# Two chained matmul steps taken in turn, one scaling write instead of two, and weight preparation moved by some ticks, in a fused attention and mixer kernel

## The chip, the cores and the metric

One core of a Trainium2 chip runs the whole program in one launch. The metric is device microseconds for one execution (lower is better), as the median of several runs. The engines are TensorE (PE in the profile, with PEld for its weight loads), VectorE (DVE), ScalarE (ACT), GpSimd (POOL) and SyncE (SP), which issues most of the DMAs.

## What is computed

The inputs are float32: q, k and v of shape (2, 8, 768, 64) and the weights of two feed-forward blocks. The reference, cut to what matters here (the attention's output x has the shape (2, 768, 512)):

```python
# 1. attention: a query sees the keys whose six hash bits (signs of q @ proj, k @ proj) are its own
scores = np.where(q_bucket == k_bucket, q @ k.T / 8, -1e9)
x = softmax(scores) @ v
# 2. first block: token shift, then
k = np.maximum(xk @ w_k, 0)
x = sigmoid(xr @ w_r) * (k * k @ w_v)
# 3. second block: gating along the sequence
h = np.maximum(x @ w_in, 0)
u, v = h[..., :512], h[..., 512:]
v_n = (v - v.mean(-1)) / np.sqrt(v.var(-1) + 1e-6)
v_s = w_spatial @ v_n + b_spatial[:, None]
out = (u * v_s) @ w_out
```

## The kernel before

Every float32 operand of a matmul is held as two fp32r parts, a high part (a cast, made by ACT) and a low part (operand less high part, a subtraction by DVE). A product is then three matmuls, high by high, high by low and low by high; `mm3` (L178) writes them for a list of chunks of 128 rows. A product over 512 rows is a group of 12 matmuls of 512 columns.

The program has two parts. `attention` issues its work in an order written out by hand (L578). `mixers` does both feed-forward blocks, and its order is set by ticks: each call of a group of matmuls ends in `tick()` (L200), which advances a counter and issues the jobs that stand in the plan for that tick, in the order in which they were put there. `at_tick(n, job)` plans a job; `later(lag, job)` plans one relative to now. All engines run their own instructions in the order of issue, so a job's tick sets its place in the queue of its engine, not its time.

The first block ends at tick 59. The second block treats the 1536 rows of x as three tiles n = 0, 1, 2 of 512 rows. It has these steps:

- `step_u(n)` (L916): four groups for the half u of `x @ w_in`, each evacuated by ACT with a Relu into XT (L920). Ticks 60 to 63 for n = 0, 64 to 67 for n = 1, 76 to 79 for n = 2.
- `step_w(n)` (L923): four groups for the half v, each evacuated by ACT into a tile `vt` (two buffers), followed by the statistics on DVE (L939, L940) and, issued at the same tick's end, `scale` (L947): a square root on ACT (L948), a reciprocal (L949) and the normalising write on DVE (L953). Ticks 68 to 75 for n = 0 and 1, 80 to 83 for n = 2.
- `step_s(b, i)` (L962): seven products of 9 matmuls of 384 columns for the mixing along the sequence, by a scheme that forms sums and differences of quarters of the operands and so needs seven block products instead of eight. Then `step_o(b, hf)` (L1020): the output products, and the DMA of the result.

The order before is u(0), u(1), w(0), w(1), u(2), w(2), then s and o (L1092 to L1134). The work that it needs is planned around it:

- `plan_split(n, ticks)` (L648) makes the operand of tile n from XT: the high part (L651, ACT) at a tick and the low part (L655, DVE) one tick later, for four chunks c. There are eight slots: tile n uses the slots 4 * (n % 2) to 4 * (n % 2) + 3, so tile 2 takes the slots of tile 0 over and can be written when both u(0) and w(0) have read them.
- `plan_in(1, ticks)` (L710) prepares the second half of `w_in`, which step w reads, in four chunks of 128 rows. `plan_weight` (L205) spreads a chunk over ticks: the load (L38) two ticks ahead, the magnitude (L42, ACT) at its tick n, clamp, shift and top (L45, L50, L56, DVE) at n + 1, first (L72, ACT), power and low (L63, L66, DVE) at n + 2, and rest (L77, L78, DVE), which writes the low half of the weight, at n + 3. The raw words lie in `w_raw`, which has two buffers: the load of chunk c waits for the low job of chunk c - 2.
- `plan_spatial(c, n)` (L826) prepares a third of `w_spatial`: two loads at n - 2 (L833) into the same two buffers of `w_raw`; at n a copy by ACT (L843) and five subtractions by DVE (L846 and L850 to L853, the plain low part and the differences of quarters); at n + 2 two copies by ACT (L860, highs) and two subtractions by DVE (L864, lows). The loads of the next third wait for these lows, one for each buffer.
- `plan_quarter` (L874) loads two more quarters of `w_spatial` at ticks 79 and 82.
- `first_part` to `seventh_part` (L1046 to L1077) form the operands of step s from the normalised quarters, at ticks 74 to 81 for batch 0 and between the groups of step o for batch 1.

The normalised v of batch b is held in four quarters a11, a12, a21 and a22 (`raw_tile`, L756, six buffers of 128 x 2 x 384). One group of step w gives 128 rows of two of them; `scale` writes them in two operations, one for each quarter, with 256 columns each. The results of matmuls go to six PSUM banks in turn (`bank`, L169).

Of the kernel before, what the change touches and what calls it, by code (L numbers as in the profile page):

```python
# [10 lines left out]
F32 = mybir.dt.float32  # L11
# [7 lines left out]
HS = S // 2  # L19
# [612 lines left out]
def mixers(tc, nc, mid, wide, top, XT, slots, parked, epsT, wr, wk, wv, w_in, w_spT, b_sp, w_out, out, split,  # L632
# [15 lines left out]
    def plan_split(n, ticks):  # L648
        for c, t in enumerate(ticks):
            def first(c=c):  # L650
                nc.scalar.copy(slots[4 * (n % 2) + c][:, 0], own(n, c))  # L651

            def rest(c=c):
                d = slots[4 * (n % 2) + c]
                nc.vector.tensor_sub(d[:, 1], own(n, c), d[:, 0])  # L655

            at_tick(t, first)
            at_tick(t + 1, rest)
# [6 lines left out]
    with tc.tile_pool(name="m1", bufs=1) as m1:  # L665
        more = m1.tile([128, 2, 2, TB], F32R, name="more")
        slots.extend(more[:, n] for n in range(2))
        k2, os, held = {}, {}, []

        def step_r(n):  # L670
            for m in range(4):
                r_group(n, m, m1, "rg", 2)

        def k_bank(i):
            if i % 4 == 3:
                return obank
            return ps_t.tile([128, 512], F32, tag="t", name="k")

        def key(i):
            n, m = divmod(i, 8)  # L680
            o = k_bank(i)
            mm3(o, [(wsl(wk, c, m), hl(slots[4 * (1 - n % 2) + c])) for c in range(4)])
            t = m1.tile([128, TB], F32, tag="kt", name="kt")
            nc.scalar.activation(t, o, AF.Relu)
            nc.scalar.square(t, t)
            k2[i] = m1.tile([128, 2, TB], F32R, tag="k2", bufs=4, name="k2")
            nc.scalar.copy(k2[i][:, 0], t)  # L687
            held.append(lambda kk=k2[i]: nc.vector.tensor_sub(kk[:, 1], t, kk[:, 0]))  # L688
            if m != 1 or n == 0:
                held.pop()()  # L690
            tick()

        def value(i):
            n, c = divmod(i, 8)
            if c == 0:
                os[n] = [ps_s.tile([128, 2, 512], F32, tag="s", name="v") for _ in range(2)]
            xh, xl = hl(k2.pop(i))
            for m in range(4):
                o = os[n][m // 2][:, m % 2, :]
                wh, wl = wsl(wv[c // 4], c % 4, m)  # L700
                for k, (w, x) in enumerate(((wh, xh), (wh, xl), (wl, xh))):
                    nc.tensor.matmul(o, w, x, start=(c == 0 and k == 0), stop=(c == 7 and k == 2))  # L702
                if c == 7 and m % 2:
                    for k in (m - 1, m):
                        nc.vector.tensor_mul(own(n, k), os[n][k // 2][:, k % 2, :], rg[n][:, k, :])
            while held:
                held.pop()()
            tick()

        def plan_in(h, ticks):  # L710
            for c, t in enumerate(ticks):
                w = wk[:, :, c, DM:] if h else wr[:, :, c, :]
                plan_weight(t, hl(w), w_in[128 * c:128 * c + 128, DM * h:DM * h + DM])

        def new_w_out():
            w_o.append(top.tile([128, 2, 2, DM], F32R, tag="x", name="w_o"))

        def plan_out(cs, ticks):
            for c, t in zip(cs, ticks):
                plan_weight(t, lambda c=c: wo(c), w_out[128 * c:128 * c + 128])  # L720

        plan_mix(2, 0, 0, (2, 3, 4, 5), nc.vector)
        plan_mix(0, 1, 4, (6, 7, 8, 9), nc.vector)
        plan_mix(1, 1, 0, (13, 15, 18, 20), nc.scalar)
        plan_in(0, (28, 31, 34, 37))
        at_tick(39, new_w_out)
        plan_out((0, 1), (40, 43))
        plan_mix(2, 1, 4, (29, 32, 35, 38), nc.scalar)
        plan_split(0, (45, 46, 47, 48))
        plan_out((2, 3), (48, 51))  # L730
        plan_in(1, (54, 56, 58, 60))
        plan_split(1, (57, 58, 60, 61))
        gates()
        r_group(0, 2, top)
        r_group(0, 3, top)
        step_r(1)
        step_r(2)
        assert now[0] == 11
        key(0)
        key(1)  # L740
        for i in range(24):
            if i < 22:
                key(i + 2)
            value(i)
        assert now[0] == 59

    with tc.tile_pool(name="m2", bufs=1) as m2:
# [5 lines left out]
        vop = {k: m2.tile([128, 2, 2, HS], F32R, name=f"v_{k}") for k in ("a11", "a12", "a22")}  # L753
        raw, w22, b11, work = {}, {}, {}, {}

        def raw_tile(dt=F32):  # L756
            return m2.tile([128, 2, HS], dt, tag="raw", bufs=6, name="raw")

        def wide_op(t, i):
            if i:  # L760
# [3 lines left out]
        def op_of(k, b, i):  # L764
            if k in vop:
                return vop[k][:, 0, i], vop[k][:, 1, i]
            if k == "s1":
                return one[:, 0, i], one[:, 1, i]
            if k == "s2":
                if b == 0:  # L770
                    t = parked[6 + i]
                elif i:
                    t = parked[3]
                else:
                    t = work["s2"]
                return t[:, 0], t[:, 1]
            return wide_op(wr if k == "s3" else wk, i)

# [137 lines left out]
        def step_u(n):  # L916
            for m in range(4):
                o = bank("u")
                mm3(o, [(wsl(wr, c, m), hl(slots[4 * (n % 2) + c])) for c in range(4)])
                nc.scalar.activation(plain(n, m), o.rearrange("p (h s) -> p h s", h=2), AF.Relu)  # L920
                tick()

        def step_w(n):  # L923
            for j in range(4):
                o = bank("w")
                js = slice(128 * j, 128 * j + 128)
                pairs = []
                for c in range(4):
                    xh, xl = hl(slots[4 * (n % 2) + c])
                    pairs.append(  # L930
                        ((xh[:, js], xl[:, js]), (wk[:, 0, c, DM:], wk[:, 1, c, DM:]))
                    )
                mm3(o, pairs)
                t = m2.tile([128, DM], F32, tag="vt", bufs=2, name="vt")
                nc.scalar.activation(t, o, AF.Relu)
                st = m2.tile([128, 6], F32, tag="st", bufs=3, name="st")
                mv = m2.tile([128, 2], F32, tag="mv", bufs=3, name="mv")
                sd = m2.tile([128, 1], F32, tag="sd", bufs=3, name="sd")
                nc.vector.bn_stats(st, t)  # L939
                nc.vector.bn_aggr(mv, st)  # L940
                b, c = divmod(4 * n + j, 6)
                names = ("a12", "a22") if c > 2 else ("a11", "a21")
                if b == 0 and c == 0:
                    for k in ("a11", "a12", "a21", "a22"):
                        raw[0, k] = raw_tile()

                def scale(t=t, mv=mv, sd=sd, b=b, c=c, names=names):  # L947
                    nc.scalar.activation(sd, mv[:, 1:2], AF.Sqrt, bias=epsT)  # L948
                    nc.vector.reciprocal(sd, sd)  # L949
                    for h, k in enumerate(names):  # L950
                        if (b, k) not in raw:
                            raw[b, k] = raw_tile()
                        nc.vector.tensor_scalar(  # L953
                            raw[b, k][:, :, 128 * (c % 3):128 * (c % 3) + 128],
                            t[:, 256 * h:256 * h + 256].rearrange("p (i n) -> p i n", i=2),
                            mv[:, 0:1], sd, op0=ALU.subtract, op1=ALU.mult,
                        )

                later(1, scale)
                tick()  # L960

# [96 lines left out]
        def fourth_part(b):  # L1058
            low("s1", b)
            s2_sum(b)  # L1060
            low("a11", b)
            for i in range(2):
                high("s2", b, i)
# [13 lines left out]
                low("s3", b, i)  # L1077

        for c in range(3):
            plan_spatial(c, (64, 66, 69)[c])  # L1080
        plan_split(2, (71, 72, 73, 73))
        h21, l21, _ = plan_quarter(lambda t, c: wr[:, t, c, :HS], 0, 79)
        h22, l22, s22 = plan_quarter(lambda t, c: wk[:, t, c, DM:DM + HS], HS, 82)
        for n, job in zip(
# [5 lines left out]
        at_tick(82, l21)  # L1090
        turn[0] += 1
        step_u(0)  # L1092
        step_u(1)
        step_w(0)
        step_w(1)
        step_u(2)
        step_w(2)
        assert now[0] == 83
        t = raw_tile()
        work.update(a=t[:, 0], b=t[:, 1], u=s22[1][:, HS:])  # L1100

        def before_first():
# [8 lines left out]
        step_s(0, 0, before_first, within_first)  # L1111
        step_s(0, 1, middle=lambda: low("s4", 0, 1))

        def more_sums():
            work["s2"] = raw_tile(F32R)
            fourth_part(1)

        def last_sums():
            for i in range(2):
                high("s4", 1, i)  # L1120
# [6 lines left out]
            fifth_part(1)  # L1127

        step_o(0, 0, (lambda: first_part(1), lambda: second_part(1), lambda: third_part(1)))
        step_o(0, 1, (more_sums, next_sums, last_sums))  # L1130
        step_s(1, 0)
        step_s(1, 1)
        step_o(1, 0)
# [67 lines left out]
```

## Time and profile before

| | |
|---|---|
| median of 3 runs | 535.88 us (532.23 to 537.28) |
| the profiled execution | 530.72 us, span 528.6 us |
| PE busy in it | 520.0 us, 98% of the span |
| DVE busy | 416.9 us, 79% |
| ACT busy | 331.6 us, 63% |
| POOL busy | 148.2 us, 28% |
| granted clock of TensorE | 1.0 over the span |

The profile is of one execution. Its span runs from the first instruction to the last, and the time of the execution has some 2 us around it. The rows further down are from its trace: each names an engine, a line of the kernel, the operation, output and input tile, and times in us from the start of the span. A value in brackets with an arrow is the time that the engine sat idle before that instruction, and what released it. An engine's instructions overlap a little where the next one doesn't read what the last one wrote, so the distance of two starts can be less than a duration.

### The profile page before, as it was taken

The page shows a single profiled execution, that of the slowest core. Times are in us where ns is not written, and L with a number is a line of the kernel's source. Part 1 is how long each engine was busy: PE and PEld are TensorE (multiplying, and loading weights), DVE is VectorE, ACT ScalarE, POOL GpSimd, SP SyncE. Part 2 cuts the span into 40 slices and gives each one's busy share as a digit, 9 for nine tenths or more (in the row PEclk, how much of TensorE's full clock was granted, in tenths as well). Part 3 has the DMA queues.
Part 4 walks back from the last instruction along what each step waited for, and adds up shares of the span by engine and source line. Part 5 has one row for each costly group of instructions (what it writes and reads, how often), then busy time and mean ns, then how long its engine had stood idle before and what let it go on. Part 6 is the DMA issues. An engine that isn't in the chain of part 4 may idle for free.

```text
span 528.6 us, 8305 instructions
## 1 busy us (share of the span) xinstructions
PE 520.0 (98%) x2850; PEld 417.1 (79%) x2850; DVE 416.9 (79%) x861; ACT 331.6 (63%) x682; POOL 148.2 (28%) x159
## 2 busy tenths in 40 slices
PE   8999999999999999999999999999999979999997
PEld 6778676868677776688888888888888858998996
DVE  8787898888989789989678687856885898977750
ACT  8888788878788687566666567554444455326121
POOL 7859766776785441100000000000000000210300
PEclk9999999999999999999999999999999999999999
DMA  8986876686859310301211121212221200103002
GB/s 237 190 181 145 191 192 139 151 196 180 165 141 171 90 64 16 96 1 41 79 55 66 42 79 42 79 40 81 80 91 60 91 14 1 46 1 116 5 20 101
DMA packets 20042, 49.88 MB, mean 94 GB/s; under 512 B 3776, under 2 KB 7424, under 8 KB 20000
## 3 DMA queue, kind: packets, MB, share of 16 engines
q1 hardware_dynamic: 14288, 32.35, 20.2%
q0 software_dynamic: 5280, 16.71, 15.1%
q8 instruction: 23, 0.38, 0.3%
q10 hardware_dynamic: 432, 0.28, 0.2%
q14 instruction: 19, 0.16, 0.1%
HBM read 45.11 MB, written 3.19 MB: 91 GB/s over the span
## 4 chain that ended last, share of the span: by engine, by line
PE 86%; DVE 6%; DMA 5%; ACT 2%; issue 1%; SPq 0%; DVEq 0%; ACTq 0%
PE v L702 12%; PE o L183 12%; PE o L462 11%; PE t L427 11%; PE s L395 11%; PE k L183 9%; PE s L183 7%; PE r L183 6%; PE u L183 4%; PE w L183 2%; DVE p L405 1%; DMA rb<-ds 1%; DMA wst<-in_w_spT_dram 1%; DMA w_raw<-in_w_r_dram 1%; DMA x<-in_kq_dram 1%
## 5 line engine op out<-in xcount | busy, mean ns | idle before, releaser
L405 DVE TENSOR_SCALAR_CACHE_REDUCE p<-s 128x768 f32<-128x768 f32 x96 | 91.2, 952 | 17.0 <-PE s L395 11.9
L417 ACT ACTIVATE p<-p,m 128x768 f32<-128x768 f32 x96 | 90.1, 940 | 13.8 <-DVE p L405 12.9
L395 PE MATMUL s<-tk 128*128 128x384 f32 x384 | 87.0, 357 | 0.1
L131 POOL TENSOR_TENSOR tk<-g,tk 128x384 fp32r<-128x384 f32 x8 | 9.2, 1155 | 273.8 <-ACT tk L130 270.1
L427 PEld LDWEIGHTS t<-ident,p 128*128 128x128 f32 x576 | 65.8, 140 | 19.7 <-ACT p L417 4.9
L427 PE MATMUL t<-ident,p 128*128 128x128 f32 x576 | 80.2, 276 | 0.7 <-ACT PT L433 0.4
L433 ACT COPY PT<-t 128x384 f32<-128x384 f32 x146 | 64.7, 475 | 21.4 <-PE t L427 21.4
L702 PE MATMUL v<-k,wv 128*128 128x512 f32 x288 | 68.9, 389 | 0.0
L462 PE MATMUL o<-PT,v 128*64 128x384 f32 x384 | 66.4, 492 | 0.4 <-DVE XT L474 0.4
L395 PEld LDWEIGHTS s<-tk 128*128 128x128 f32 x384 | 62.6, 189 | 2.7 <-POOL tk L341 0.6
L702 PEld LDWEIGHTS v<-k,wv 128*128 128x128 f32 x288 | 54.1, 188 | 11.2
L276 POOL TENSOR_TENSOR tk<-x,tk 64x384 fp32r<-64x384 f32 x56 | 57.8, 1051 | 10.8 <-DMA tk<-in_kq_dram 9.5
L462 PEld LDWEIGHTS o<-PT,v 128*64 128x64 f32 x384 | 25.8, 137 | 31.6 <-issue 30.2
L688 DVE TENSOR_TENSOR k<-kt,k 128x512 fp32r<-128x512 f32 x24 | 16.6, 690 | 24.8 <-ACT k L687 24.6
L183 PE MATMUL k<-tk,wk 128*128 128x512 f32 x144 | 35.6, 389 | 0.0
L183 PEld LDWEIGHTS k<-tk,wk 128*128 128x128 f32 x144 | 27.0, 188 | 5.6
L130 ACT CAST tk<-g 128x384 fp32r<-128x384 f32 x16 | 8.2, 513 | 36.4 <-DVE g L973 36.4
L156 DVE SCALAR_TENSOR_TENSOR f<-XT,msc,d 128x256 f32<-128x256 f32 x48 | 24.1, 503 | 6.5 <-ACT d L150 5.1
L183 PE MATMUL w<-wk,tk 128*128 128x512 f32 x114 | 26.5, 389 | 0.0
L433 DVE COPY PT<-t 128x384 f32<-128x384 f32 x46 | 24.7, 547 | 2.1 <-PE t L427 2.0
L183 PE MATMUL r<-tk,wr 128*128 128x512 f32 x108 | 25.7, 392 | 0.0
L183 PEld LDWEIGHTS w<-wk,tk 128*128 128x128 f32 x114 | 21.4, 188 | 4.4
(194 smaller groups left out, 933.5 us busy)
## 6 DMA issues: line engine op xcount, KB each, us to landing
tk<-in_kq_dram POOLq DMA_DIRECT2D x30, 384.0 KB, 7.8
x<-in_kq_dram POOLq DMA_DIRECT2D x6, 768.0 KB, 5.0
w_raw<-in_w_k_dram SPq DMA_DIRECT2D x8, 512.0 KB
w_raw<-in_w_v_dram SPq DMA_DIRECT2D x8, 512.0 KB
w_raw<-in_w_in_dram SPq DMA_DIRECT2D x8, 512.0 KB
v<-in_vP_dram SPq DMA_DIRECT2D x8, 384.0 KB
rb<-ds SPq DMA_DIRECT2D x30, 96.0 KB
out_dram<-ot SPq DMA_DIRECT2D x11, 256.0 KB
```

Of the source, the lines that this page charges most:

```text
L131: (eng or nc.vector).tensor_sub(lo, src, hi)
L156: nc.vector.scalar_tensor_tensor(st["f"], x, mu, st["d"], op0=ALU.mult, op1=ALU.add)
L183: nc.tensor.matmul(o, a, x, start=(i == 0), stop=(i == len(seq) - 1))
L276: nc.gpsimd.tensor_sub(tk[l, 1 + 2 * t, o], raw[pp][l, t, o], tk[l, 2 * t, o])
L395: nc.tensor.matmul(s[:, c, :HS], w, t[:, n, c * HS:(c + 1) * HS], start=(n == 0), stop=(n == 1),)
L405: nc.vector.tensor_scalar(c, s[:, :, :HS], -0.125, BIG / 16, op0=ALU.mult, op1=ALU.min, accum_out=m)
L417: nc.scalar.activation(c, c, AF.Exp, bias=m, scale=-1.0, accum_out=den[g][:, u:u + 1])
L427: nc.tensor.transpose(t[:, 128 * n:128 * n + 128], p[:, k0:k0 + 128], ident)
L433: copy(PT[g][:, e, 3 * c:3 * c + 3, 128 * j:128 * j + 128], t[:, :HS].rearrange("p (n q) -> p n q", n=3),)
L462: nc.tensor.matmul(obank[64 * e:64 * e + 64, :HS], vt[g // 2][:, kt, e, :], PT[g][:, e, kt, :], start=(kt == 0), stop=(kt == 5),)
L688: held.append(lambda kk=k2[i]: nc.vector.tensor_sub(kk[:, 1], t, kk[:, 0]))
L702: nc.tensor.matmul(o, w, x, start=(c == 0 and k == 0), stop=(c == 7 and k == 2))
```

## The change

The steps u and w alternate: u(0), w(0), u(1), w(1), u(2), w(2). The plan follows: the last chunk of the second half of `w_in` comes a tick earlier, the splits of tile 1 come four ticks later, those of tile 2 one or two ticks earlier (three of the four), and the second and third part of the spatial weights one and two ticks later. The normalised quarters of one group lie side by side in one tile of four (three buffers of double size), and one operation of 512 columns writes what two of 256 wrote. The scratch of step s is the half of such a tile that held a12 of batch 0, and the first s2 operand of batch 1 lies in a parked slot instead of a raw tile.

```diff
@@ mixers @@
-        plan_in(1, (54, 56, 58, 60))
-        plan_split(1, (57, 58, 60, 61))
+        plan_in(1, (54, 56, 58, 59))
+        plan_split(1, (61, 62, 64, 65))
...
-        def raw_tile(dt=F32):
-            return m2.tile([128, 2, HS], dt, tag="raw", bufs=6, name="raw")
+        def raw_tile():
+            return m2.tile([128, 4, HS], F32, tag="raw", bufs=3, name="raw")
@@ op_of @@
                 if b == 0:
                     t = parked[6 + i]
-                elif i:
-                    t = parked[3]
                 else:
-                    t = work["s2"]
+                    t = parked[1 + 2 * i]
@@ step_w @@
-                if b == 0 and c == 0:
-                    for k in ("a11", "a12", "a21", "a22"):
-                        raw[0, k] = raw_tile()
-
                 def scale(t=t, mv=mv, sd=sd, b=b, c=c, names=names):
                     nc.scalar.activation(sd, mv[:, 1:2], AF.Sqrt, bias=epsT)
                     nc.vector.reciprocal(sd, sd)
-                    for h, k in enumerate(names):
-                        if (b, k) not in raw:
-                            raw[b, k] = raw_tile()
-                        nc.vector.tensor_scalar(
-                            raw[b, k][:, :, 128 * (c % 3):128 * (c % 3) + 128],
-                            t[:, 256 * h:256 * h + 256].rearrange("p (i n) -> p i n", i=2),
-                            mv[:, 0:1], sd, op0=ALU.subtract, op1=ALU.mult,
-                        )
+                    if c % 3 == 0:
+                        raw[b, c] = raw_tile()
+                        for h, k in enumerate(names):
+                            raw[b, k] = raw[b, c][:, 2 * h:2 * h + 2]
+                    nc.vector.tensor_scalar(
+                        raw[b, c - c % 3][:, :, 128 * (c % 3):128 * (c % 3) + 128],
+                        t.rearrange("p (k n) -> p k n", k=4),
+                        mv[:, 0:1], sd, op0=ALU.subtract, op1=ALU.mult,
+                    )
@@ mixers @@
-            plan_spatial(c, (64, 66, 69)[c])
-        plan_split(2, (71, 72, 73, 73))
+            plan_spatial(c, (64, 67, 71)[c])
+        plan_split(2, (69, 70, 72, 73))
...
         step_u(0)
+        step_w(0)
         step_u(1)
-        step_w(0)
         step_w(1)
         step_u(2)
         step_w(2)
         assert now[0] == 83
-        t = raw_tile()
+        t = raw[0, "a12"]
...
-        def more_sums():
-            work["s2"] = raw_tile(F32R)
-            fourth_part(1)
...
-        step_o(0, 1, (more_sums, next_sums, last_sums))
+        step_o(0, 1, (lambda: fourth_part(1), next_sums, last_sums))
```

## Rows read from the trace of the kernel before

**Rows 1.** The page, busy time of each engine over the span.
```profile
PE 520.0 (98%) x2850; PEld 417.1 (79%) x2850; DVE 416.9 (79%) x861; ACT 331.6 (63%) x682; POOL 148.2 (28%) x159
```

**Rows 2.** Waits of PE: who waited for whom, us in total, times, longest.
```profile
PE u L183 <- DVE tk L655: 2.7, 3, 1.3
PE o L285 <- POOL ident masks.py:199: 1.3, 1, 1.3
```

**Rows 3.** PE in order of time, 375 to 452 us: start, us, engine, line, what.
```profile
379.51 2.88 PE L183 MATMUL u<-tk,wr 128*128 128x512 f32 x12
382.24 2.88 PE L183 MATMUL o<-tk,wr 128*128 128x512 f32 x12
...
423.04 0.39 PE L183 MATMUL u<-tk,wr 128*128 128x512 f32 x1
423.60 0.97 PE L183 MATMUL u<-tk,wr 128*128 128x512 f32 x3 [0.17 <-DVE tk L655]
425.84 0.96 PE L183 MATMUL u<-tk,wr 128*128 128x512 f32 x3 [1.27 <-DVE tk L655]
428.08 6.90 PE L183 MATMUL u<-tk,wr 128*128 128x512 f32 x29 [1.28 <-DVE tk L655]
...
448.42 1.75 PE L183 MATMUL s<-b,v_a 128*128 128x384 f32 x9
```

**Rows 4.** DVE in order of time, 365 to 456 us.
```profile
374.57 0.69 DVE L66 SCALAR_TENSOR_TENSOR w_a<-w_raw,w_p 128x512 f32<-128x512 uint32 x1
...
379.29 0.68 DVE L655 TENSOR_TENSOR tk<-XT,tk 128x512 fp32r<-128x512 f32 x1
...
391.31 0.68 DVE L655 TENSOR_TENSOR wk<-XT,wk 128x512 fp32r<-128x512 f32 x1
...
392.64 0.69 DVE L78 TENSOR_TENSOR wk<-w_b,w_a 128x512 fp32r<-128x512 f32 x1
...
404.76 0.56 DVE L846 TENSOR_TENSOR b<-wst,b 128x384 fp32r<-128x384 f32 x1 [2.83 <-ACT b L843]
...
407.61 0.69 DVE L939 BATCH_NORM_STATS2 st<-vt 128x6 f32<-128x512 f32 x1
...
408.43 1.80 DVE L864 TENSOR_TENSOR wsp<-wst,wsp 128x768 fp32r<-128x768 f32 x2
...
410.40 0.73 DVE L953 TENSOR_SCALAR raw<-vt,mv,sd 128x256 f32<-128x256 f32 x2
...
422.89 0.66 DVE L655 TENSOR_TENSOR tk<-XT,tk 128x512 fp32r<-128x512 f32 x1
...
425.12 0.66 DVE L655 TENSOR_TENSOR tk<-XT,tk 128x512 fp32r<-128x512 f32 x1
...
427.36 1.26 DVE L655 TENSOR_TENSOR tk<-XT,tk 128x512 fp32r<-128x512 f32 x2
...
441.14 0.70 DVE L939 BATCH_NORM_STATS2 st<-vt 128x6 f32<-128x512 f32 x1 [1.12 <-ACT vt L935]
```

**Rows 5.** ACT in order of time, 365 to 456 us.
```profile
378.88 0.68 ACT L42 ACTIVATE w_a<-w_raw 128x512 f32<-128x512 f32 x1
...
404.22 0.51 ACT L843 CAST b<-wst 128x384 fp32r<-128x384 f32 x1 [3.41 <-DMA wst<-in_w_spT_dram]
...
412.33 0.51 ACT L843 CAST b<-wst 128x384 fp32r<-128x384 f32 x1 [1.68 <-DMA wst<-in_w_spT_dram]
```

**Rows 6.** The chain that ended last, 380 to 530 us: start, us, what.
```profile
401.09 3.10 DMA wst<-in_w_spT_dram
...
409.38 2.93 DMA wst<-in_w_spT_dram
```

**Rows 7.** DVE's groups by line and shape: count, busy us, mean ns, idle before.
```profile
L45 DVE TENSOR_SCALAR w_a<-w_a 128x512 f32<-128x512 f32 x32 | 15.6, 489 | 0.0
...
L953 DVE TENSOR_SCALAR raw<-vt,mv,sd 128x256 f32<-128x256 f32 x24 | 8.8, 410 | 0.4
...
L152 DVE TENSOR_SCALAR d<-XT,omu 128x256 f32<-128x256 f32 x24 | 8.4, 349 | 0.4
```

## The prediction

> **What bounds the kernel now.** I read the page's busy shares first: PE is busy for 520.0 of 528.6 us and every other engine for less than 80% [rows 1]. Where PE never rests, only two things can shorten the run: less work for PE, or the removal of a wait of PE. The change takes no matmul away, so the second view is the list of what PE waited for. Its longest entry is 2.7 us, in three waits of the products u for the subtraction at L655, the split of the operand tiles; the next is 1.3 us, in the matmuls that warm PE at the start (L285), and what follows is smaller still [rows 2].
>
> The third view, PE in order of time, places them. A group of 12 matmuls takes 2.72 us: the first starts at 379.51, the second at 382.24 [rows 3]. Steps u and w are 24 such groups, so 65.3 us without a wait, and step s would start at 379.51 + 65.3 = 444.8. It starts at 448.42 [rows 3]. The 3.6 us lost all lie in the first group of step u(2): 1, 3 and 3 matmuls stand at 423.04, 423.60 and 425.84, each piece ending in a wait for one more chunk's low half, and from 428.08 PE runs on without a pause [rows 3]. (The list gives 2.7 us because the matmul before a wait is drawn longer than its place in the pipe; the starts give the whole loss.)
>
> The fourth view, DVE in order of time, says why the splits are late. The four of tile 2 are written at 422.89, 425.12, 427.36 and straight after, between statistics and scalings of w(1) [rows 4]. DVE runs from 404.76 to there almost without a pause; the wait before 404.76 was 2.83 us for ACT [rows 4], which itself stood 3.41 us for a load of the spatial weights, and again 1.68 us before 412.33 [rows 5]. The two loads took 3.10 and 2.93 us from the release of their buffer [rows 6]. So DVE has the work of eight w groups and of spatial chunks 1 and 2 pressed into the 20 us before u(2), and PE overtakes it there. It catches up later: at 441.14 it waits 1.12 us for ACT in the first group of w(2) [rows 4]. After that PE shows no wait to the end [rows 2], so a microsecond saved before u(2) is a microsecond of the whole.
>
> **The new order.** w(0) comes before u(1). Tile 0's slots are then free after group 8 instead of 12 and can take tile 2 four groups earlier, and w(0)'s work for DVE moves from 404 on to 394 on. I walk DVE's queue in the new order with the durations of the trace, PE's groups at 2.72 us from 379.51. (The same walk over the order of before starts s at 448.3 against 448.42, so the method is good to about 0.2 us.)
>
> **Weights for w(0).** They are wanted 10.9 us earlier: w(0) starts at 379.51 + 4 x 2.72 = 390.39, and its eleventh matmul, the first that reads the low half of chunk 3, at 392.66. Before, that half was written from 392.64 to 393.33, behind an unbroken queue which held four splits of tile 1, the first at 379.29 and the last at 391.31 [rows 4]. The change puts those splits behind it. Four times 0.60 is 2.4 us, so it is done at 390.9 to 391.1, 1.6 us in hand. The magnitude of chunk 3 is a tick earlier on ACT. Its load still waits for chunk 1's product to free a buffer, which ends just after 379.3, where the split follows it [rows 4]. A load of this size took 3.6 us at most (chunk 0's product ends at 374.57 + 0.69, chunk 2's magnitude starts at 378.88) [rows 4, 5], so the magnitude runs from 383.0, and DVE comes to it at 385.7. ACT stands there for about 3.5 us with the evacuation of u(0)'s first group behind it; PE has six banks in turn and is 16 us from wanting that one back. Cost: nothing. If the load took over 7.2 us, PE would wait for the excess.
>
> **Splits of tile 1.** All four now end by 401.9 in the walk; u(1) starts at 401.27 and wants the last low half at its eleventh matmul, 403.5. In hand 1.6 us, cost nothing.
>
> **The merged scaling.** Two 128x256 writes take 0.73 us together [rows 4], 0.41 each [rows 7]. No row shows one of 128x512 with two per-partition scalars. Lower bound 0.42, the clamp at that size with immediates, in this stretch (its mean over the run is 0.49 [rows 7]). Upper bound 0.81: 0.69 for the statistics over the same 512 columns [rows 4], plus 0.12 for two scalars (0.41 against 0.35 for the form with one gives 0.06 each [rows 7]). I take 0.54: 0.41 less 0.12 is 0.29 for 256 columns with immediates, against 0.42 for 512, so 256 more columns cost 0.13. It is nearest to the clamp, the same operation on the same kind of operand. The gain is 0.2 us in each of 12 groups, all on DVE.
>
> [...]
>
> **Splits of tile 2, the term that decides.** Units on DVE in this stretch: five spatial subtractions take 2.85 us (404.76 to 407.61), a group's statistics 0.82 (to 408.43), the two lows 1.77, the first 0.95 (1.80 to the end of the second), reciprocal and scaling 0.84 to the next start (from 410.2; the pair ends at 411.13), now 0.65, a split 0.6 [rows 4]. From 393.9, when the first group of w(0) is evacuated, the walk goes: statistics, chunk 0's subtractions, three groups of w(0) and the last two splits of tile 1 to 401.8; lows of chunk 0, the first ending at 402.7. That frees the buffer; 3.1 us of load [rows 6] and 0.5 us of copy on ACT later, at 406.4, chunk 1's subtractions begin, then a scaling and the lows, the first ending at 410.8. Split 0 is done at 412.3. Load and copy again, 414.5. From there 2.85 (subtractions), split 1 (done at 418.0), statistics 0.82, 0.4 for ACT's square root, scaling 0.65, statistics 0.82, lows 1.77, and split 2 ends at 423.0; scaling, statistics, and split 3 ends at 425.05. PE wants split 2 at 424.63 and split 3 at 425.31 (u(2) starts at 423.04 and reads these at its 8th and 11th matmul). So nothing is late, with 1.6 and only 0.25 us in hand. The third spatial chunk two ticks later and the second one tick later cost nothing by themselves: they spread the same work out, and step s reads it from 444.8 on.
>
> **What is late next.** DVE comes to the first group of w(2) with 1.1 us to wait for ACT, as before, so all later steps stand to PE as they did. The other edits cost nothing: the scratch of s, now the buffer half of a12, and the first s2 operand of batch 1, now in a parked slot, are free long before they are written, and neither adds an instruction. No load changes size.
>
> **Sum.** 3.6 us saved, less 0.1 for the thin margin of split 3, so 3.5 us. The profiled execution took 530.72 us (span 528.6), so 527.2. It is 5.2 us below the median of the runs shown, 535.88, and below the lowest, 532.23; I take the saving from the median: 532.4.
>
> **Rivals.**
> *A part of the stall stays.* The chain to split 3 has 0.25 us in hand, and holds five scalings and two loads. If the merged write took 0.81, five times 0.27 less 0.25 is 1.1 us of stall, a saving of 2.5: 533.4. If both loads took 0.5 us longer, 0.75 us of stall: 533.0. For it: the margin is less than the scatter of a load (3.10 and 2.93). Against it: nothing in the rows says that either is slower than I took it.
> *Saved and given back.* Step s could wait for DVE, ACT or the quarter loads of spatial weights, since PE comes 3.6 us earlier: 535.9. Against it, DVE's 1.12 us of rest before w(2) [rows 4], and that those loads are issued by PE's own ticks.
> *Weights late for w(0).* Point 7.2 us of load for chunk 3; at 9 us the loss is 1.8 and the time 534.1. Against it the 3.6 us above.
> *Slower.* The two loads of the spatial weights lie in series in DVE's queue, each freed by DVE's own lows and each ahead of the splits of u(2). Every microsecond on each costs two. From (3.6 + 0.25)/2 = 1.9 us more, so 5.0 us a load, the saving is gone; at 6.0 us the stall is 5.55 and the kernel is 2 us slower: 537.8. For it, that ACT is seen to wait for exactly these loads [rows 5]; against it, 3.10 and 2.93 us [rows 6].
>
> **How the numbers follow.** Forecast 0.66; part of the stall stays 0.18; given back 0.06; weights late 0.04; slower 0.06. A measurement of this kernel tells about 1%, 5.4 us, from no change: the three runs lie between 3.7 below and 1.4 above their median. The forecast is 0.65%, so same. A measured gain over 1% needs 1.9 us of luck on top: I give it a fifth of the forecast's 0.66 and little of the rest, 0.15. Slower by over 1% needs the last rival and bad luck, 0.03. Range: 532.4 less about 3.4 of scatter, 529.0; on the other side the given-back case with 1.4 on it, 537.3.
>
> **What would show it.** Right: PE lists no wait for L655, or one under 0.5 us; step s starts 65.3 to 65.8 us after u(0); the merged write shows 0.54 us; split 3 of tile 2 ends close to 425. Wrong: a wait in the first group of w(0) or u(1), a wait of PE in step s that wasn't there, or the first group of u(2) still in pieces.

## The result and the profile after

The changed kernel takes 527.11 us in the median of 6 runs (526.79 to 528.12), the kernel before 532.49 in 6 runs that include the three shown above. The ratio on record is 0.9882, with a 95% interval of 0.9841 to 0.9923 (the two medians alone give 0.9899). The forecast was 532.4 us with a range from 529.0, so the measured time lies 1.9 us below the range, and the saving is 5.4 us where 3.5 were forecast.

The profiled execution of the changed kernel took 527.00 us, its span is 525.2. The sum that the prediction made against the profiled execution before was 527.2. So the working, put on that execution, was right to 0.2 us, and the time forecast was not; the experiments say why.

The page, busy time (answers to [rows 1]): PE's busy share goes from 98% to 99%, and DVE has 12 instructions less.
```profile
PE 518.6 (99%) x2850; PEld 416.9 (79%) x2850; DVE 413.6 (79%) x849; ACT 331.3 (63%) x682; POOL 149.4 (28%) x159
```
The waits of PE (answers to [rows 2]; who waited for whom, us in total, times, longest). The 2.7 us of u for L655 are gone. Nothing stands in their place: L285 is the start, L427 and L462 are lines of the attention.
```profile
PE o L285 <- POOL ident masks.py:199: 1.3, 1, 1.3
PE t L427 <- ACT PT L433: 0.8, 1, 0.8
PE o L462 <- DVE XT L474: 0.6, 1, 0.6
```
PE in order of time (answers to [rows 3]). The 36 matmuls of u(2)'s first three groups are one piece now. Step s starts 445.10 - 379.66 = 65.44 us after u(0), against 68.91 before: 3.47 us less.
```profile
379.66 2.88 PE L183 MATMUL u<-tk,wr 128*128 128x512 f32 x12
...
390.54 8.32 PE L183 MATMUL w<-wk,tk 128*128 128x512 f32 x36
...
423.18 8.48 PE L183 MATMUL u<-tk,wr 128*128 128x512 f32 x36
431.50 2.88 PE L183 MATMUL o<-tk,wr 128*128 128x512 f32 x12
...
445.10 1.75 PE L183 MATMUL s<-b,v_a 128*128 128x384 f32 x9
```
DVE in order of time (answers to [rows 4]; L948 and L937 are L953 and L939 of before). The low half of chunk 3 of w(0)'s weight is written from 390.50, the last split of tile 1 from 401.45, the four of tile 2 from 411.98, 417.58, 422.65 and 424.72. The whole is 0.15 us later than the walk's time base, since u(0) starts at 379.66.
```profile
390.50 0.69 DVE L78 TENSOR_TENSOR wk<-w_b,w_a 128x512 fp32r<-128x512 f32 x1
...
398.12 0.55 DVE L948 TENSOR_SCALAR raw<-vt,mv,sd 128x512 f32<-128x512 f32 x1
...
401.45 0.66 DVE L655 TENSOR_TENSOR wk<-XT,wk 128x512 fp32r<-128x512 f32 x1
...
406.74 0.56 DVE L844 TENSOR_TENSOR b<-wst,b 128x384 fp32r<-128x384 f32 x1 [1.42 <-ACT b L841]
...
411.98 0.68 DVE L655 TENSOR_TENSOR tk<-XT,tk 128x512 fp32r<-128x512 f32 x1
414.70 0.56 DVE L844 TENSOR_TENSOR b<-wst,b 128x384 fp32r<-128x384 f32 x1 [2.04 <-ACT b L841]
...
417.58 0.68 DVE L655 TENSOR_TENSOR tk<-XT,tk 128x512 fp32r<-128x512 f32 x1
...
422.65 0.68 DVE L655 TENSOR_TENSOR tk<-XT,tk 128x512 fp32r<-128x512 f32 x1
...
424.72 0.66 DVE L655 TENSOR_TENSOR tk<-XT,tk 128x512 fp32r<-128x512 f32 x1
...
438.11 0.69 DVE L937 BATCH_NORM_STATS2 st<-vt 128x6 f32<-128x512 f32 x1 [1.10 <-ACT vt L933]
```
ACT in order of time (answers to [rows 5]; L841 is L843 of before): it stands 3.62 us ahead of chunk 3's magnitude, where about 3.5 were foreseen, and it still stands for the loads.
```profile
383.26 0.68 ACT L42 ACTIVATE w_a<-w_raw 128x512 f32<-128x512 f32 x1 [3.62 <-DVE wk L78]
...
406.19 0.52 ACT L841 CAST b<-wst 128x384 fp32r<-128x384 f32 x1 [3.76 <-DMA wst<-in_w_spT_dram]
...
414.16 0.51 ACT L841 CAST b<-wst 128x384 fp32r<-128x384 f32 x1 [1.00 <-DMA wst<-in_w_spT_dram]
```
DVE still rests for these loads as well, 1.42 and 2.04 us in the rows above. What the new order changes is the time before them. From 394.15 to 405.32 DVE now works on w(0)'s groups and the first spatial chunk without a pause; in the kernel before it rested there twice, 2.83 us before 404.76 and, in a row not shown so far,
```profile
400.11 1.83 DVE L864 TENSOR_TENSOR wsp<-wst,wsp 128x768 fp32r<-128x768 f32 x2 [2.77 <-ACT wsp L860]
```
DVE's groups (answers to [rows 7]): the merged write takes 0.547 us.
```profile
L948 DVE TENSOR_SCALAR raw<-vt,mv,sd 128x512 f32<-128x512 f32 x12 | 6.6, 547 | 0.4
```

### The profile page after: what moved, and what is told of

It is laid out like the page before. It is cut to its first block, busy times and chain, and to the rows that moved or that the text cites. A ratio compares the mean times of both kernels' runs of the same rounds, so it can differ in the third digit from the quotient of the medians.

```text
span 525.2 us, 8294 instructions
## 1 busy us (share of the span) xinstructions
PE 518.6 (99%) x2850; PEld 416.9 (79%) x2850; DVE 413.6 (79%) x849; ACT 331.3 (63%) x682; POOL 149.4 (28%) x159
## 4 chain that ended last, share of the span: by engine, by line
PE 93%; DMA 3%; DVE 2%; ACT 1%; issue 0%; SPq 0%; DVEq 0%
PE o L183 13%; PE v L702 12%; PE o L462 12%; PE t L427 11%; PE s L395 11%; PE k L183 9%; PE s L183 7%; PE r L183 6%; PE u L183 5%; PE w L183 5%; DMA rb<-ds 1%; DMA w_raw<-in_w_r_dram 1%; DVE p L405 1%; PE z L293 1%; DMA ds<-rt 1%; DVE tk L380 1%
## 5 line engine op out<-in xcount | busy, mean ns | idle before, releaser
L427 PEld LDWEIGHTS t<-ident,p 128*128 128x128 f32 x576 | 65.8, 140 | 19.9 <-ACT p L417 5.0
L427 PE MATMUL t<-ident,p 128*128 128x128 f32 x576 | 80.1, 275 | 1.0 <-ACT PT L433 0.8
L462 PE MATMUL o<-PT,v 128*64 128x384 f32 x384 | 66.3, 491 | 0.6 <-DVE XT L474 0.6
L276 POOL TENSOR_TENSOR tk<-x,tk 64x384 fp32r<-64x384 f32 x56 | 59.4, 1079 | 8.6 <-DMA tk<-in_kq_dram 6.4
L462 PEld LDWEIGHTS o<-PT,v 128*64 128x64 f32 x384 | 25.8, 136 | 31.7 <-issue 30.2
L42 ACT ACTIVATE w_a<-w_raw 128x512 f32<-128x512 f32 x32 | 21.7, 678 | 6.6 <-DVE wk L78 3.6
L66 DVE SCALAR_TENSOR_TENSOR w_a<-w_raw,w_p 128x512 f32<-128x512 uint32 x32 | 23.5, 734 | 1.0
```

Of the source, the lines that this page charges most:

```text
L42: nc.scalar.activation(st["a"].bitcast(F32), st["raw"][:, :, 1].bitcast(F32), AF.Abs)
L66: nc.vector.scalar_tensor_tensor(st["a"].bitcast(F32), st["raw"][:, :, 0], 2.0 ** -52, st["p"].bitcast(F32), op0=ALU.mult, op1=ALU.mult,)
L276: nc.gpsimd.tensor_sub(tk[l, 1 + 2 * t, o], raw[pp][l, t, o], tk[l, 2 * t, o])
L427: nc.tensor.transpose(t[:, 128 * n:128 * n + 128], p[:, k0:k0 + 128], ident)
L462: nc.tensor.matmul(obank[64 * e:64 * e + 64, :HS], vt[g // 2][:, kt, e, :], PT[g][:, e, kt, :], start=(kt == 0), stop=(kt == 5),)
```

## The experiments

Two things were open: which part of the change does the work, and where the 1.9 us come from by which the measured saving exceeds the forecast. Beside its time, each run gives the mean granted clock of TensorE over its span; a run "keeps the clock" when that is 0.999 or 1.000. For the stage I give "u to s": from the start of u(0) to the start of step s, 68.91 us before and 65.44 after.

**The kernel before, again** (unchanged).

> The kernel before, unchanged, against itself. Theory (the trace's 530.72 us is what this kernel takes, and the runs of 535.88 and 537.28 were strays): most of its runs lie at 530.5 to 533 us, the span of the profiled one near 528.6, ratio 1.00. Rival (its stall before step u(2) varies with the load of the spatial weights, so the kernel itself scatters and the traced run was a lucky one): runs spread over 531 to 537 us, and a profile of a longer one shows the first group of step u(2) more than 3.6 us late.

12 runs, 530.38 to 540.65, median 532.26, ratio 1.0002 (0.9979 to 1.0026). The clock sorts them: three runs at 530.4 to 530.9 kept it, seven at 532.0 to 533.1 have 0.997, two are longer, at 0.990 and 0.987. This profile is of a run with 0.997. PE in order of time, u(2) and its sequel:
```profile
423.70 0.39 PE L183 MATMUL u<-tk,wr 128*128 128x512 f32 x1
424.27 0.96 PE L183 MATMUL u<-tk,wr 128*128 128x512 f32 x3 [0.18 <-DVE tk L655]
426.50 0.96 PE L183 MATMUL u<-tk,wr 128*128 128x512 f32 x3 [1.28 <-DVE tk L655]
428.75 8.47 PE L183 MATMUL u<-tk,wr 128*128 128x512 f32 x29 [1.27 <-DVE tk L655]
```
The ratio and most of the times are as the theory had them, but the profiled span is 530.8 and not near 528.6. The waits are those of [rows 3] to 0.01 us, so the rival's reason falls: the stall doesn't grow. But the 29 matmuls behind it take 8.47 us instead of 6.90. Busy time by stretch in the same run (us, then PE, PEld, DVE, ACT, POOL, granted clock, DMA share, GB/s) shows the clock at 0.54 from 428.75 to 432.50; in steps of 1 us from 429 it is 0.52, 0.50, 0.50, 0.77 and, from 433, 1.00. So it stood for some 3 us at 0.50, half of the 1.00 around it:
```profile
424.00:426.00 2.00, 1.05 (x4) 0.49 (x3) 1.93 (x7) 1.57 (x4) 0.00 (x0) 1.00 0.06 23
426.00:428.75 2.75, 0.97 (x4) 0.49 (x4) 2.68 (x8) 2.11 (x4) 0.00 (x0) 1.00 0.00 0
428.75:432.50 3.75, 3.75 (x10) 2.94 (x11) 3.07 (x8) 2.34 (x6) 0.00 (x0) 0.54 0.00 0
432.50:434.00 1.50, 1.50 (x8) 1.24 (x7) 1.46 (x4) 0.52 (x1) 0.00 (x0) 1.00 0.00 0
```
In the profile on which the prediction rests the same stretch is at 1.00 throughout:
```profile
426.00:428.00 2.00, 0.80 (x3) 0.32 (x3) 1.97 (x6) 1.36 (x3) 0.00 (x0) 1.00 0.00 0
428.00:432.00 4.00, 3.92 (x17) 3.25 (x18) 3.33 (x9) 2.43 (x6) 0.00 (x0) 1.00 0.00 0
```
So a new theory: the broken activity in u(2) makes TensorE's clock fall behind it in most runs, and that costs another 1.57 us. The rows show the fall behind the third wait, to 0.52 and 0.50, and the return to 1.00 by 433; what decides on either they don't show. And the same waits left the clock at 1.00 in the profile of before, so the fall is no certain consequence of them.

**Order and ticks without the merged write.** Against the kernel before, all of the change's ticks and the order of steps, and nothing else:
```diff
...
-        plan_split(2, (71, 72, 73, 73))
+        plan_split(2, (69, 70, 72, 73))
...
         step_u(0)
+        step_w(0)
         step_u(1)
-        step_w(0)
```


> The change without the merged write (two operations of 256 columns, six raw tiles): order of steps and all ticks as in the changed kernel. Theory (DVE's queue up to split 3 of tile 2 sets the time): five scalings before that split cost 0.19 us more each, of which 0.25 us was in hand; a wait of 0.7 us in the first group of u(2), step s 0.7 us later than in the changed kernel, 2.7 us less than before. Rival (the free slots alone make the gain): no wait in u(2), 3.5 us less than before.

Median 527.67 (ratio 0.9900, 0.9863 to 0.9937), all six runs with the clock kept. One wait is left, for split 3 as expected, of 0.86 us where 0.7 were expected; u to s is 66.44, that is 2.5 us less than before and 1.0 more than in the changed kernel. So DVE's queue sets the time, not the free slots alone.
```profile
422.77 2.43 PE L183 MATMUL u<-tk,wr 128*128 128x512 f32 x10
426.06 6.19 PE L183 MATMUL u<-tk,wr 128*128 128x512 f32 x26 [0.86 <-DVE tk L655]
```

**The merged write alone.** Against the changed kernel, the old order and all old ticks:
```diff
...
-        plan_split(2, (69, 70, 72, 73))
+        plan_split(2, (71, 72, 73, 73))
...
         step_u(0)
-        step_w(0)
         step_u(1)
+        step_w(0)
```


> The kernel before with the merged write alone: old order, old ticks, raw tiles of four quarters. Theory (DVE's queue): the write takes 0.55 us, and the splits of tile 2 come 0.9 us earlier, so 2.6 us of stall are left in u(2): 0.9 us less than before. Rival (the free slots alone): stall and time as before.

Median 529.71 (ratio 0.9939, 0.9909 to 0.9968). Two waits of 1.05 and 1.08 us are left. This profile too is of a run that lost its clock (29 matmuls in 8.46 us); without that 1.56 us, u to s is 69.61 - 1.56 = 68.05, 0.9 us less than before, as expected. 5 of the 12 runs lost the clock, against 9 of the 12 above. That would fit a smaller stall that costs the clock less often, but 12 runs each don't show it.

**The new order without the spread.**
```diff
-            plan_spatial(c, (64, 67, 71)[c])
+            plan_spatial(c, (64, 66, 69)[c])
```


> The changed kernel with the ticks of the spatial weights put back to 64, 66, 69. Theory (DVE's queue with two loads in series): the second and third part, which then stand a tick and two ticks earlier, take DVE ahead of the splits of tile 2, and ACT stands for each load; splits 2 and 3 come 2.9 us late in all, so only 0.6 us less than before. Rival (the free slots alone): 3.5 us less, as the changed kernel.

Median 531.15, not told from before (0.9989, 0.9954 to 1.0024); u to s is the surer measure here. It is 68.35, 0.56 us less than before: waits of 1.41 and 1.09 us for splits 2 and 3. DVE stands 2.78 and 2.67 us for the two copies that wait for loads. The order frees the slots, and the spatial weights take the time back; the rival falls. 7 of 12 runs lost the clock.

**The waits filled with matmuls.** In the kernel before, 13 matmuls more in u(2)'s first group, whose result, in the unused half of another tile, nobody reads:
```diff
-                mm3(o, [(wsl(wr, c, m), hl(slots[4 * (n % 2) + c])) for c in range(4)])
+                if n == 2 and m == 0:
...
+                        nc.tensor.matmul(o, wh, xh, start=(c == 0), stop=False)
+                        for j in range((1, 6, 6, 0)[c]):
+                            nc.tensor.matmul(
+                                fill[:, 1, :], wh, slots[4 * (n % 2)][:, 0], start=True, stop=True
+                            )
+                        nc.tensor.matmul(o, wh, xl, start=False, stop=False)
...
```


> The kernel before with 13 matmuls more in the first group of u(2), of the chunk's weight and the first slot's high half into an unused half bank that nobody reads: 1, 6 and 6 of them ahead of the three matmuls that wait for a split. They take 0.23 us each, so they fit into the waits. Theory (PE's broken activity in that group makes the chip halve TensorE's clock behind it in most runs, which costs 1.6 us): step s starts as late as before, 68.9 us after u(0), but the clock stays at 1.0 in all runs: 530.5 to 531.5 us, some 1.5 us below the median of before. Rival (the loss of clock has another cause): most runs at a mean clock of 0.997 and 532.4 us, as before.

u to s is 68.96, the stall untouched, and all 12 runs kept the clock: 530.23 to 531.95, median 530.89, 1.5 us below the 532.40 of the kernel before beside it, of whose 24 runs 17 lost it (0.9976, 0.9955 to 0.9997). That is the test of the new theory: with work in the gaps the clock stayed in 12 runs of 12, with the gaps empty and the same work late it fell in 17 of 24. Busy time by stretch:
```profile
424.00:426.00 2.00, 2.00 (x10) 1.38 (x8) 1.93 (x7) 1.57 (x4) 0.00 (x0) 1.00 0.01 2
426.00:428.00 2.00, 2.00 (x10) 1.55 (x9) 1.97 (x5) 1.36 (x3) 0.00 (x0) 1.00 0.00 0
428.00:432.00 4.00, 4.00 (x19) 3.13 (x18) 3.32 (x9) 2.52 (x6) 0.00 (x0) 1.00 0.00 0
```

**The old order with buffers of their own for the loads of the second part of the spatial weights.**
```diff
-                t = mid.tile([128, 512, 2], U32, tag="w_raw", bufs=2, name="wst")
-                st[k] = t.rearrange("p a b -> p (a b)")[:, :S].bitcast(F32)
+                if c == 1:
+                    st[k] = raw_tile().rearrange("p t n -> p (t n)")
+                else:
+                    t = mid.tile([128, 512, 2], U32, tag="w_raw", bufs=2, name="wst")
+                    st[k] = t.rearrange("p a b -> p (a b)")[:, :S].bitcast(F32)
```


> The kernel before, old order, with the loads of the second part of the spatial weights in two raw tiles that are free then, so that neither the second nor the third part's load waits for DVE's lows. Theory (DVE's queue with two loads in series): DVE no longer stands for the loads (2.8 and 0.9 us); the four splits of tile 2 end at 420, 422, 424.6 and 425.2 us, in time for u(2) with 0.1 us or less in hand; no wait or one under 0.5 us, step s 3.0 to 3.5 us earlier, clock 1.0 in all runs, 527 to 528 us, as the changed kernel. Rival (tile 2's slots come free too late in the old order, whatever the loads): the wait stays over 2 us and the time over 530 us.

Median 527.87 (0.9925, 0.9902 to 0.9949), clock kept in all six runs. u to s is 65.55, 3.4 us less. The last splits come 2.8 us sooner than in [rows 4], though u(0) starts 0.5 us later and order and writes are the old ones, and PE waits for none:
```profile
402.39 0.55 DVE L849 TENSOR_TENSOR b<-raw,b 128x384 fp32r<-128x384 f32 x1
...
410.10 0.54 DVE L849 TENSOR_TENSOR b<-wst,b 128x384 fp32r<-128x384 f32 x1
...
424.57 1.26 DVE L655 TENSOR_TENSOR tk<-XT,tk 128x512 fp32r<-128x512 f32 x2
```
The subtractions at 402.39 and 410.10 have no wait before them; in [rows 4] the first stood 2.83 us. So taking these loads out of DVE's queue is enough to end the stall in the old order: tile 2's slots come free in time there too, and the new order is one of two cures.

**The merged write twice**, in the changed kernel:
```diff
+                    nc.vector.tensor_scalar(
+                        raw[b, c - c % 3][:, :, 128 * (c % 3):128 * (c % 3) + 128],
+                        t.rearrange("p (k n) -> p k n", k=4),
+                        mv[:, 0:1], sd, op0=ALU.subtract, op1=ALU.mult,
+                    )
```


> The changed kernel with the merged write issued twice, the same values to the same place, 0.47 us more for DVE in each of 12 groups. Theory (DVE's queue; 0.25 us in hand and five scalings ahead of split 3): 2.2 us of wait in the first group of u(2), in two pieces of 0.3 and 1.9 us; step s 2.2 us later than in the changed kernel. Clock: lost in some runs, since the wait is like that of the merged write alone; median 529.3, single runs to 531. Rival (DVE isn't what u(2) waits for): no wait, 527.1 us.

The waits came for the splits named, 0.86 and 1.67 us, and u to s is 68.39, 2.95 us more than in the changed kernel against 2.2 expected: the second write starts 0.58 us after the first, where 0.47 were taken for it. Step s then has a wait of 0.4 us more. The median, 531.51 (0.9993, 0.9976 to 1.0010), is 2.2 us over the expectation: four of the five runs with the clock kept take 530.4 to 530.9 (the fifth 532.41), and 7 of 12 lost it.

**The changed kernel again, with its margin widened and without.** Two rounds of the unchanged kernel, and one version with the loads of the second part in a raw tile, issued at tick 62:
```diff
+                if c == 1:
+                    if not k:
+                        st["both"] = raw_tile()
+                    st[k] = st["both"][:, 2 * k:2 * k + 2].rearrange("p t n -> p (t n)")
...
-            at_tick(n - 2, lambda: load(0))
-            at_tick(n - 2, lambda: load(1))
+            early = 62 if c == 1 else n - 2
+            at_tick(early, lambda: load(0))
+            at_tick(early, lambda: load(1))
```


> The changed kernel, unchanged. Theory: no wait of PE from 379 us on, clock at 1.0 in all runs, 526.8 to 528.2 us, 5 us below the median of before: 3.5 us of stall and about 1.6 us of clock in most runs of before. Rival (the difference of the medians beyond 3.5 us was chance): 528.5 to 529 us.

> The changed kernel with the two loads of the second part of the spatial weights into a raw tile that is free then, issued at tick 62, so that no load but the first waits for DVE's lows. Theory (DVE's queue with two loads in series): DVE waits for no load but that of the third part, split 3 of tile 2 ends 1.1 us sooner and has 1.3 us in hand instead of 0.25; PE had no wait there already, so the median stays at 527.1 us, but the odd run with a mean clock of 0.997 (530.2 us, 2 of 13 so far) is gone: all runs at 526.6 to 528.2 us. Rival (those odd runs come from elsewhere): some runs at 530 us again.

> The changed kernel, unchanged, beside e9 on the same chip. Theory: median 527.1 us, one or two runs of 530 us at a mean clock of 0.997, where a load came late for a split with 0.25 us in hand. Rival: none.

The changed kernel: 527.07 in 7 runs (0.9922, 0.9895 to 0.9950) and 526.64 in 6 (0.9883, 0.9854 to 0.9911, the runs of before beside it at 532.62). With the first six, 17 of 19 runs kept the clock; two, both in the first of these rounds, took 530.2 and 530.4 at 0.997, where all were expected to keep it; in the second round one or two such runs were expected and none came. With the loads moved, split 3 ends 1.2 us before PE wants it, against 0.07 us in the changed kernel. The median is then 526.75, the same, and two of nine runs are long, so the expectation that they would vanish fell. One of the two was profiled. It has no wait of PE in this stage (u to s 65.28), but one in the attention, where a load of the softmax denominators (L455) came late:
```profile
PE o L462 <- DVE XT L474: 5.1, 2, 4.7
```
The mean granted clock is 1.00 from 104 to 120 us of that run, 0.61 from 120 to 122 and 0.50 from 122 to 126, so the clock fell behind that wait of 4.71 us as well; the load took 8.76 us in its chain. So this stray comes from a part that is the same in both kernels. The other long runs of the changed kernel and those of the kernel before (537 us and more) were not profiled; whether they have the same cause stays open.

## Why the prediction was right and wrong

**Right: the bound, the stall and its cause.** All of the 3.6 us lay in u(2)'s first group, and 3.47 us of it went. The change acts through DVE's queue: order and ticks alone give 2.5 us, the merged write alone 0.9, the new order without the spread 0.56, and taking the loads out of the queue 3.4 in the old order. Neither the order with its ticks nor the merged write does it alone, and the order needs the spread; the spread alone was not run.

**Right: the walk.** Chunk 3's low half was forecast to be done at 390.9 to 391.1 and is at 391.19; splits 2 and 3 at 423.0 and 425.05, and they end at 423.33 and 425.38 on a time base 0.15 us later. Of the 0.25 us in hand for split 3, 0.07 were left, and u to s is 65.44 against 65.3 without a wait. The merged write cost 0.547 us, for 0.54; the bound of 0.81 is out. What was costed at nothing cost nothing, and DVE's rest before w(2) is 1.10 us for 1.12.

**Wrong: "I take the saving from the median: 532.4".** I put the saving on 535.88, a median of three runs of which two (535.88, 537.28) were strays; six runs give 532.49. This step alone is 3.4 of the 5.3 us by which the forecast is off. That two of three runs were that long was bad luck: of 79 more runs of this kernel 6 took 535.88 or more. But all three were above the profiled execution, by 1.5 to 6.6 us, and I noted that and passed it over as scatter. Taken from the profiled execution the time would have been 527.2, within 0.1 us of the measured median.

**Wrong: a term was missing from the sum.** The step that failed is "only two things can shorten the run: less work for PE, or the removal of a wait of PE", and with it "a microsecond saved before u(2) is a microsecond of the whole". There is a third thing, TensorE's clock behind the wait (0.50 for some 3 us in the kernel before, profiled again), which the sum put at nothing without asking. "3.6 us saved" is what the stall costs in a run that keeps its clock. Of 79 runs of the kernel before beside these experiments 18 did, with a median of 530.84; the profiled one was such a run, with a mean clock of 1.000. The other 61, at a mean clock of 0.997 (41 runs) or lower, have a median of 532.90. In the one of them that was profiled, as in the profiled run of the merged write alone, the clock falls behind the stall, and that adds 1.57 us. The changed kernel has no stall and keeps its clock in 17 of 19 runs.

The 5.4 us between the medians come out so. The stall is worth 3.5 us: in runs that keep the clock, the median span goes from 528.7 to 525.2. The clock is worth about 1.5, the difference of the median of all 79 runs, 532.40, to the 530.84. The last 0.35 us lie outside the span: an execution takes 2.15 us more than its span in the kernel before and 1.80 in the changed one, and no experiment was made for that. The prediction gave a gain of over 1% a chance of 0.15, by "1.9 us of luck"; 1.9 us did come on top, but most of it came from the clock. No row before the result shows the clock fall. The sign was there that all three timed runs were slower than the profiled one, at a clock of 1.0 and with 7 matmuls in the 5 us of the stall, and the prediction never asked what the clock does behind that in the others.

**The rivals.** Late weights, a stall given back and a slower kernel did not occur. The part that stays is what the experiments without the merged write and without the spread show.

## What to carry to other kernels

A short broken stretch of TensorE can cost more than its idle time. Here it cost 3.5 us, and another 1.57 in the run whose clock was then at 0.50 for some 3 us: look for the granted clock after each stall in several executions, not in the one profiled, and compare the runs' mean clocks before taking a base. When the profiled execution is faster than every timed run, ask what the others have that it hasn't, and don't put a sum made on the one on the median of the others. When an engine's queue waits for loads whose buffers it frees itself, as DVE's did for 2.83 us before 404.76, a free buffer elsewhere may do what a new order of steps does: u to s was 65.55 us with the buffers and 65.44 with the changed kernel.

## What the runs showed of the hardware that was not expected

Behind three waits of 0.18, 1.28 and 1.27 us, ahead of which stood 1, 3 and 3 matmuls, the granted clock fell to 0.50 for some 3 us in one profiled run, and in the other it stayed at 1.00 behind the same waits (alike to 0.01 us). The kernel whose profile has a single wait of 0.86 us kept the clock in six runs of six; the one with two of 1.05 and 1.08 us lost it in 5 of 12. With 13 unread matmuls in the three waits the clock stayed in 12 runs of 12.
